# VectorE and ScalarE in program order, and the bf16 identity from GpSimd, in a windowed-attention and mixture-of-depths kernel

## The chip, the cores and the metric

The kernel runs on one core of a Trainium2 chip. The metric is the device time of one execution in microseconds. The five engines are named as the profile names them: PE (TensorE, with PEld for its weight loads), DVE (VectorE), ACT (ScalarE), POOL (GpSimd) and SP (SyncE, which here only issues transfers).

## What is computed

Sliding-window attention with sink tokens, followed by a small expert layer that only the best-scored rows of each batch go through. Batch 4, 8 heads, sequence 768, head size 64, 4 sink tokens, window 128, 128 rows chosen per batch.

```python
def _attn_ref(q, k, v, n_sink, window):
    scores = scale * np.matmul(q, k.transpose(0, 1, 3, 2))
    ...
    keep = is_sink | in_window
    scores = np.where(keep, scores, -1000000000.0)
    ...
    a = a / (np.sum(a, axis=-1, keepdims=True) + 1e-09)
    return np.matmul(a, v).astype(np.float32)

def _moe_ref(x, w_gate, w1, w2, capacity):
    scores = np.einsum('bsd,d->bs', x, w_gate)
    out = x.copy()
    for b in range(B):
        top_idx = np.argpartition(-scores[b], capacity)[:capacity]
        xe = x[b, top_idx]
        h = np.maximum(xe @ w1, 0.0)
        ye = h @ w2
        g = 1.0 / (1.0 + np.exp(-scores[b, top_idx]))
        out[b, top_idx] = x[b, top_idx] + g[:, None] * ye
    return out.astype(np.float32)
```

`x` is the attention output with the heads side by side, 512 wide.

## The kernel before

**Units.** The main loop runs over 24 units, one for each batch b and block j of 128 query rows (`units`, six per batch). A unit u does the following in program order. At j == 0 the loads of the next batch are issued (`load_qk`, `load_v`), and at u0 those of three of the four weight pieces (`load_w`; the fourth at u6). Then `scores` for the *next* unit: PE multiplies K and Q (L257), adds the mask by a product with the bf16 identity (L268), and ACT takes the exponentials into `pt` (L274, four per unit). Then `pv_sinks` and `pv` for this unit: PE sums the products with V in PSUM tiles `xg` (L291, L301), in two halves of four heads, and DVE normalises each half (L307 reciprocal of the row sum, L310 multiplication into `x`). At j == 0 `sink_scores` (L280, L282) follows. `transposes` turns one or two head pairs of the next batch (PE L227, DVE copies KT at L232 and two small pieces ksk at L236, ACT copies QT at L234). In batch 1 `cast_w` casts two weight pieces per unit on ACT (L212, L215), in the units j = 0 to 3. `compare` ranks the *previous* unit: PE transposes its column of gate scores (L324), ACT copies it (L325), DVE counts (L328). One step of the generator `moe_steps` of the previous batch follows. Last comes `finish_block`: the store of `x` (L315) and the gate score of each row as a dot product on DVE (L317).

**The expert steps.** `moe_steps` of batch b runs spread over the units of batch b+1, one step per unit from j == 1: the ranks (L340, L344, L345), the selection matrix E (L347) and the row numbers (L352, L353); the indices (L359, L362), the gate (L364 to L366) and the gather of the chosen rows by an indirect transfer (L369); their transposition (L375, L377); the first product (L385, L387); the second product (L391, L394) and the indirect transfer that adds to the output (L395). For the last batch all steps run at the end, one after the other.

**Loads.** All loads and the stores of `x` are issued by SP. `load_v` has a DVE instruction in its middle: after the second of six pieces of V it loads the sink rows (`vsr`, L126, two small transfers) and multiplies them by a selection pattern into `vsk` (L127). For batch 0 this stands ahead of the main loop; for batches 1 to 3 it stands at the head of unit u0, u6 and u12. The casts of q and k to bf16 are made by ACT and DVE in batch 0 (L107, L108) and by POOL afterwards (L111, an affine_select that changes no value).

**Buffers.** `xg` has three PSUM buffers, two used per unit; the other PSUM tiles share five. `x` has four buffers, each free when its store has landed. The f32 tiles of q and k have three buffers per kind, two used per batch; the bf16 ones three. V has one buffer for even and one for odd batches.

**What sets the order.** The framework places each instruction in its engine's stream when the program is built. For an engine that is named in `manual_schedule` the instructions within that block keep the order of the program. For the others a planner takes, by its own estimate of times, the first instruction of the program whose inputs are ready. Before the change only PE is named, so DVE, ACT, POOL and SP are ordered by the planner. What stands ahead of the block (constants, masks, the loads of batch 0) is ordered by the planner in any case. On the chip each stream is executed as it stands.

The identity matrix exists twice: `ident_f` in f32, for the transposes of the gate scores (L324), and `ident_b` in bf16, for the other transposes and the masks. `make_identity` is a POOL memset followed by a POOL affine_select.

Of the kernel before, what the change touches and what calls it, by code (L numbers as in the profile page):

```python
# [10 lines left out]
BF16 = mybir.dt.bfloat16  # L11
# [4 lines left out]
ENG = mybir.EngineType  # L16
# [15 lines left out]
def kernel(  # L32
# [13 lines left out]
    nc = tc.nc  # L46

    cp = ctx.enter_context(tc.tile_pool(name="cp", bufs=1))
# [24 lines left out]
    def keep_warm(n):  # L73
        w = ps.tile([128, 512], FP32, name="w", tag="ps")
        for _ in range(n):
            nc.tensor.matmul(out=w[:, :], lhsT=warm[:, 0:128], rhs=warm[:, :], start=True, stop=True)
# [21 lines left out]
    def casts(st, hp):  # L98
        kb = qbp.tile([128, 2, NB, D], BF16, name="kb", tag="kb")
        qb = qbp.tile([128, 2, NB, D], BF16, name="qb", tag="qb")  # L100
        h0 = 2 * (hp % 2)
        ks = st.kf[hp // 2][:, h0:h0 + 2, :, :].rearrange("p h c d -> p (h c d)")
        qs = st.qf[hp // 2][:, h0:h0 + 2, :, :].rearrange("p h c d -> p (h c d)")
        ko = kb[:, :, :, :].rearrange("p h c d -> p (h c d)")
        qo = qb[:, :, :, :].rearrange("p h c d -> p (h c d)")
        if st.b == 0:
            nc.scalar.copy(out=ko, in_=ks)  # L107
            nc.vector.tensor_copy(out=qo, in_=qs)  # L108
        else:
            for o, i in ((ko, ks), (qo, qs)):  # L110
                nc.gpsimd.affine_select(out=o, in_=i, compare_op=ALU.is_ge, fill=0.0, base=0,  # L111
                                        pattern=[[0, 2 * NB * D]], channel_multiplier=0)
        st.kq[hp] = (kb, qb)
# [17 lines left out]
    st0 = load_qk(0, 2)  # L131


    ident_f = cp.tile([128, 128], FP32, name="ident_f", tag="ident_f")
    make_identity(nc, ident_f)
    ident_b = cp.tile([128, 128], BF16, name="ident_b", tag="ident_b")
    nc.vector.tensor_copy(ident_b[:], ident_f[:])  # L137
    for i in range(2):
        nc.vector.memset(vsr[i][:, :], 0.0)
        nc.vector.memset(ksk[i][:, :, :], 0.0)  # L140
# [60 lines left out]
    def load_w(i):  # L201
        if i < 2:
            src = moe_w1[256 * i:256 * i + 256, :].rearrange("(dc p) f -> p dc f", p=128)
        else:
            src = moe_w2[512 * (i - 2):512 * (i - 2) + 512, :].rearrange("(fc p) d -> p fc d", p=128)
        wf[i] = ws.tile([128, 2048], FP32, name="wf", tag="wf")
        nc.sync.dma_start(out=wf[i][:, :].rearrange("p (a n) -> p a n", a=src.shape[1]), in_=src)  # L207
# [10 lines left out]
    def transposes(st, hp):  # L218
        if not hasattr(st, "QT"):
            st.QT = tp.tile([128, HP, S], BF16, name="QT", tag="QT")  # L220
            st.KT = tp.tile([128, HP, S], BF16, name="KT", tag="KT")
            st.ksk = ksk[st.b % 2]
        for t, (src, dst) in enumerate(((st.kq[hp][0], st.KT), (st.kq[hp][1], st.QT))):
            trp = ps.tile([128, 8, 128], BF16, name="trp", tag="ps")
            for c in range(NB):
                for e in range(2):
                    nc.tensor.transpose(out=trp[64 * e:64 * e + 64, c, :],  # L227
                                        in_=src[:, e, c, :], identity=ident_b[:])
            o = dst[:, hp, :].rearrange("d (p c) -> d p c", c=NB)
            i = trp[:, 0:NB, :].rearrange("d c p -> d p c")  # L230
            if t == 0:
                nc.vector.tensor_copy(out=o, in_=i)  # L232
            else:
                nc.scalar.copy(out=o, in_=i)  # L234
        for e in range(2):
            nc.vector.tensor_copy(  # L236
                out=st.ksk[64 * e:64 * e + 64, hp, 8 * (hp % 2) + 4 * e:8 * (hp % 2) + 4 * e + 4],
                in_=st.KT[64 * e:64 * e + 64, hp, 0:NSINK])
# [6 lines left out]
    def scores(st, kc, g):  # L245
        nq = 256 if kc + 1 < NB else 128
        if g == 0:
            st.pt[kc] = pp.tile([128, H, 256], FP32, name="pt", tag="pt")
        pt = st.pt[kc]
        sc = [ps.tile([128, 2, 256], FP32, name="sc", tag="ps") for _ in range(2)]  # L250
        for hh in range(2):
            hp = 2 * g + hh
            for kh in range(2):
                k0 = kc * 128 + 64 * kh
                q0, q1 = (64, nq) if kh else (0, nq if kc == 0 else min(nq, 192))
                for e in range(2):
                    nc.tensor.matmul(  # L257
                        out=sc[e][es[kh], hh, q0:q1], lhsT=st.KT[es[e], hp, k0:k0 + 64],
                        rhs=st.QT[es[e], hp, kc * 128 + q0:kc * 128 + q1],
                        start=(hh == 0), stop=False, skip_group_check=True)  # L260
        sq = [((2, 4), (0, 2)), ((0, 1), (3, 4))] if nq == 256 else [((0, 1), (0, 2))]
        for r, pair in enumerate(sq):
            for kh in range(2):
                s0, s1 = pair[kh]
                m0 = 2 if (s0, s1) == (0, 1) else 1 if s0 == 0 else 0
                m = msk0 if kc == 0 and kh == 0 else msk
                for e in range(2):
                    nc.tensor.matmul(  # L268
                        out=sc[e][es[kh], :, 64 * s0:64 * s1].rearrange("p h (s n) -> p h s n", n=64),
                        lhsT=ident_b[es[e], es[e]], rhs=m[es[e], :, m0:m0 + s1 - s0, :],  # L270
                        start=False, stop=(r == len(sq) - 1), skip_group_check=True)
        po = pt[:, 4 * g:4 * g + 4, :].rearrange("p (a e) n -> p e a n", e=2)
        for e in range(2):
            nc.scalar.activation(out=po[:, e, :, 0:nq], in_=sc[e][:, :, 0:nq], func=ACT.Exp, scale=0.125)  # L274
# [125 lines left out]
    def start_state(st):  # L400
        st.pt = {}
        st.cm = {}
        st.scol = sp.tile([128, NB], FP32, name="scol", tag="scol")
        st.row = sp.tile([128, NB], FP32, name="row", tag="row")
        st.sbc = sp.tile([128, S], FP32, name="sbc", tag="sbc")

    states = {0: st0}
    units = [(b, j) for b in range(B) for j in range(NB)]
    with tc.manual_schedule(engines={ENG.PE}):
        start_state(st0)  # L410
        keep_warm(14)
        for g in range(2):
            for hp in (2 * g, 2 * g + 1):
                casts(st0, hp)
                transposes(st0, hp)
                keep_warm(4)
            scores(st0, 0, g)
        gen = None
        prep = {True: {2: (0,), 3: (1, 2), 4: (3,)}, False: {1: (0,), 2: (1,), 3: (2,), 4: (3,)}}
        for u, (b, j) in enumerate(units):  # L420
            st = states[b]
            if j == 0 and b + 1 < B:
                states[b + 1] = load_qk(b + 1, 2 if b == 0 else 1)
                load_v(states[b + 1])
                if b == 0:
                    for i in range(3):
                        load_w(i)
            nxt = units[u + 1] if u + 1 < len(units) else None
            if nxt:
                if nxt[1] == 0:  # L430
                    start_state(states[nxt[0]])
                for g in range(2):
                    scores(states[nxt[0]], nxt[1], g)
            pv_sinks(st, j)
            hps = prep[b == 0].get(j, ()) if b + 1 < B else ()
            for hp in hps:
                casts(states[b + 1], hp)
            for g in range(2):
                pv(st, j, g)
            if j == 0:  # L440
                sink_scores(st)
            for hp in hps:
                transposes(states[b + 1], hp)
            if b == 1 and j < 4:
                cast_w(2 * j)
                cast_w(2 * j + 1)
                if j == 0:
                    load_w(3)
            if u:
                pb, pj = units[u - 1]  # L450
                compare(states[pb], pj)
            if gen is not None:
                if next(gen, "end") == "end":
                    gen = None
            finish_block(st, j)
            if j == 0 and b > 0:
                gen = moe_steps(states[b - 1])
        compare(states[B - 1], NB - 1)
        for _ in moe_steps(states[B - 1]):
            pass  # L460
# [35 lines left out]
```

The softmax here doesn't subtract the row's maximum and nothing guards it: scores larger than these inputs give would overflow.

## Time and profile before

The time is 171.62 us, the median of three runs (170.14 to 174.56). The profiled execution has a span of 173.3 us.

| engine | busy us | share of the span |
|---|---|---|
| PE (matmul) | 129.0 | 74% |
| DVE | 96.8 | 56% |
| ACT | 87.4 | 50% |
| POOL | 35.1 | 20% |

The DMA engines move 31.67 MB. No engine is busy for the whole span, so the shares do not name a bound: the table of windows, which gives busy time, granted PE clock and DMA share by stretch, and the chain of waits, which follows the last instruction back through what released it, are the views to read. Two groups matter for the change. ACT spends 46.8 us in 96 exponentials. DVE spends 20.3 us in the multiplications of L310, 17.4 in the dot products of L317, 17.9 in the counts of L328 and 15.1 in the copies of L232; the sink multiplication L127 runs four times at 0.42 us.

In the chain, 16% of the span is PE in L301; 24% is waiting for transfers.

### The profile page before, as it was taken

The numbers are of one execution on the slowest core, as the hardware profiler recorded it, in microseconds if no ns is written. First come the engines' busy times: TensorE is split into PE (matmuls) and PEld (weight loads), VectorE is DVE, ScalarE is ACT, GpSimd is POOL, SyncE is SP. The second block draws the span as 40 slices with busy tenths as digits, with TensorE's granted clock in tenths as the row PEclk, the third lists the DMA queues.
The fourth block names the chain that finished last, engine by engine and source line by source line (L and its number), as shares of the span: only waits on it lengthen the run. The fifth ranks groups of instructions, "written<-read, shape, count | busy, mean of one in ns | idle before, by whom it ended". The sixth has DMA issues, their size and how long they took to land.

```text
span 173.3 us, 6858 instructions
## 1 busy us (share of the span) xinstructions
PE 129.0 (74%) x3010; PEld 99.4 (57%) x3010; DVE 96.8 (56%) x303; ACT 87.4 (50%) x173; POOL 35.1 (20%) x51
## 2 busy tenths in 40 slices
PE   7379977589409979644999899999999699512930
PEld 2145666377207768532986678788678588201800
DVE  3188453977204999861277689775678735720000
ACT  3256873644593854646074855658585543101210
POOL 6000027600001616300541330200210200310030
PEclk9999999999755999996599999999999999955585
DMA  5999999899999799999869971311161411142004
GB/s 178 296 338 200 148 333 371 180 222 313 297 377 333 219 345 185 168 348 379 299 211 229 209 213 61 46 60 64 64 121 64 99 61 66 61 61 30 0 0 61
DMA packets 40078, 31.67 MB, mean 183 GB/s; under 512 B 26096, under 2 KB 34800, under 8 KB 40048
## 3 DMA queue, kind: packets, MB, share of 16 engines
q1 hardware_dynamic: 38896, 29.66, 59.3%
q0 software_dynamic: 1152, 1.57, 6.7%
q8 instruction: 23, 0.38, 0.9%
q14 instruction: 7, 0.06, 0.1%
HBM read 24.41 MB, written 7.34 MB: 183 GB/s over the span
## 4 chain that ended last, share of the span: by engine, by line
PE 35%; DMA 24%; DVE 13%; SPq 12%; issue 9%; ACT 2%; POOLq 1%
PE xg L301 16%; DMA xe<-out_dram,idx 9%; DMA qf<-in_q_dram 8%; DMA out_dram<-x 7%; SPq L120 6%; PE xg L291 3%; PE sc L257 3%; PE hps L385 3%; PE ye L391 3%; DVE x L310 3%; DVE KT L232 3%; SPq L126 2%; DVE cm L328 2%; SPq L207 2%; PE sc L268 2%
## 5 line engine op out<-in xcount | busy, mean ns | idle before, releaser
L274 ACT ACTIVATE pt<-sc 128x512 f32<-128x512 f32 (+1 forms) x96 | 46.8, 578 | 10.6 <-PE sc L268 10.5
L301 PEld LDWEIGHTS xg<-vbuf,pt 128*64 128x64 f32 x1408 | 46.1, 144 | 9.0 <-issue 7.0
L301 PE MATMUL xg<-vbuf,pt 128*64 128x65 f32 x1408 | 49.7, 231 | 0.6 <-PE xg L301 0.6
L307 DVE RECIPROCAL rz<-xg 128x4 f32<-128x4 f32 x48 | 8.7, 181 | 32.6 <-PE xg L301 32.5
L310 DVE TENSOR_TENSOR x<-xg,rz 128x256 f32<-128x256 f32 x48 | 20.3, 424 | 9.0 <-DMA out_dram<-x 7.4
L257 PE MATMUL sc<-QT,KT 64*64 64x192 bf16 (+3 forms) x384 | 19.3, 250 | 6.6 <-DVE KT L232 3.4
L234 ACT COPY QT<-trp 128x768 bf16<-128x768 bf16 x16 | 12.7, 799 | 22.1 <-PE trp L227 22.1
L111 POOL TENSOR_SCALAR_AFFINE_SELECT kb<-kf 128x768 bf16<-128x768 f32 x12 | 10.2, 865 | 63.6 <-DMA kf<-in_k_dram 37.9
L268 PE MATMUL sc<-msk,ident_b 64*64 64x256 bf16 (+1 forms) x352 | 17.3, 248 | 3.2 <-issue 3.2
L328 DVE SCALAR_TENSOR_TENSOR cm<-sbc,scol,tie 128x128 bf16<-128x128 f32 (+5 forms) x24 | 17.9, 747 | 2.9 <-ACT sbc L325 2.7
L317 DVE CUSTOM_DVE_ANT_0 junk<-x,wgb 128x512 f32<-128x512 f32 x24 | 17.4, 726 | 2.3 <-DMA wgb<-in_moe_w_gate_dram 2.2
L257 PEld LDWEIGHTS <-KT 64*64 64x64 bf16 x384 | 9.5, 107 | 12.6 <-issue 10.0
L291 PE MATMUL xg<-vsk,psk 64*64 64x260 f32 x128 | 12.6, 416 | 5.2 <-DVE x L310 5.2
L232 DVE COPY KT<-trp 128x768 bf16<-128x768 bf16 x16 | 15.1, 950 | 1.0 <-PE trp L227 0.9
L395 POOL DMA_INDIRECT out_dram<-gye,idx x4 | 6.4, 1589 | 42.3 <-DMA out_dram<-x 15.4
L268 PEld LDWEIGHTS <-ident_b 64*64 64x64 bf16 x352 | 10.8, 109 | 3.7 <-issue 3.7
L325 ACT COPY sbc<-bc 128x128 f32<-128x128 f32 x24 | 6.5, 271 | 12.5 <-PE bc L324 12.5
L111 POOL TENSOR_SCALAR_AFFINE_SELECT qb<-qf 128x768 bf16<-128x768 f32 x12 | 10.8, 915 | 6.1 <-PE xg L301 3.3
L227 PE MATMUL trp<-ident_b,kb 128*64 128x128 bf16 x192 | 8.7, 223 | 4.1 <-DVE ident_b L137 3.8
L375 PE MATMUL xeT<-ident_b,xe 128*128 128x128 bf16 x16 | 2.0, 264 | 11.9 <-DMA xe<-out_dram,idx 11.9
L227 PEld LDWEIGHTS <-kb 128*64 128x64 bf16 x192 | 6.8, 113 | 5.6 <-issue 5.0
L385 PE MATMUL hps<-xeT_sb,w_sb 128*128 128x128 bf16 x128 | 9.4, 242 | 0.7 <-ACT xeT_sb L377 0.7
(72 smaller groups left out, 138.9 us busy)
## 6 DMA issues: line engine op xcount, KB each, us to landing
vbuf<-in_v_dram SPq DMA_DIRECT2D x24, 256.0 KB, 5.6
out_dram<-x SPq DMA_DIRECT2D x24, 256.0 KB, 5.3
wf<-in_moe_w_dram SPq DMA_DIRECT2D x4, 1024.0 KB, 7.8
kf<-in_k_dram SPq DMA_DIRECT2D x8, 384.0 KB, 8.8
qf<-in_q_dram SPq DMA_DIRECT2D x8, 384.0 KB, 8.4
kf<-in_k_dram SPq DMA_DIRECT2D x4, 768.0 KB
qf<-in_q_dram SPq DMA_DIRECT2D x4, 768.0 KB, 4.8
wgb<-in_moe_w_gate_dram SPq DMA_DIRECT2D x1, 256.0 KB
```

Source lines behind the costliest of these rows:

```text
L111: nc.gpsimd.affine_select(out=o, in_=i, compare_op=ALU.is_ge, fill=0.0, base=0, pattern=[[0, 2 * NB * D]], channel_multiplier=0)
L227: nc.tensor.transpose(out=trp[64 * e:64 * e + 64, c, :], in_=src[:, e, c, :], identity=ident_b[:])
L232: nc.vector.tensor_copy(out=o, in_=i)
L257: nc.tensor.matmul(out=sc[e][es[kh], hh, q0:q1], lhsT=st.KT[es[e], hp, k0:k0 + 64], rhs=st.QT[es[e], hp, kc * 128 + q0:kc * 128 + q1], sta ...
L268: nc.tensor.matmul(out=sc[e][es[kh], :, 64 * s0:64 * s1].rearrange("p h (s n) -> p h s n", n=64), lhsT=ident_b[es[e], es[e]], rhs=m[es[e], ...
L274: nc.scalar.activation(out=po[:, e, :, 0:nq], in_=sc[e][:, :, 0:nq], func=ACT.Exp, scale=0.125)
L291: nc.tensor.matmul(out=st.xg[g][es[m], :, :], lhsT=st.psk[es[g], q0:q0 + 64], rhs=st.vsk[es[g], :, :], start=True, stop=False, skip_group_ ...
L301: nc.tensor.matmul(out=xg[es[m], hh, :], lhsT=st.pt[kc][:, h, off + 64 * m:off + 64 * m + 64], rhs=st.v[:, kc, h, :], start=(j < 2 and hh ...
L310: nc.vector.tensor_tensor(out=st.x[:, 256 * g:256 * g + 256].rearrange("p (h d) -> p h d", h=4), in0=xg[:, :, 0:D], in1=rz[:, :, :].to_bro ...
L317: nc.vector.tensor_tensor_reduce(out=junk[:, :], in0=st.x[:, :], in1=wgb[:, :], scale=1.0, scalar=0.0, op0=ALU.mult, op1=ALU.add, accum_ou ...
L328: nc.vector.scalar_tensor_tensor(out=cm[:, :], in0=st.sbc[:, 0:n], scalar=st.scol[:, j:j + 1], in1=tie[:, S - n:S], op0=ALU.subtract, op1= ...
L385: nc.tensor.matmul(out=hps[:, f4, :], lhsT=w1_sb[:, dc, f0:f0 + 128], rhs=xeT_sb[:, dc, :], start=(dc == 0), stop=(dc == 3))
```

## The change

Two edits. The bf16 identity is now built by POOL itself, ahead of the f32 one, and the DVE cast that made it is gone. And DVE and ACT join PE in `manual_schedule`: within the prologue of batch 0 and the main loop they execute their instructions in the order in which the program has them. The aim is that the author, and not the planner's estimate, says which copy, count or exponential goes first; the identity is built elsewhere so that the first transposes don't depend on where a DVE cast is placed. No arithmetic changes.

```diff
@@ -131,10 +131,10 @@
     st0 = load_qk(0, 2)
 
 
+    ident_b = cp.tile([128, 128], BF16, name="ident_b", tag="ident_b")
+    make_identity(nc, ident_b)
     ident_f = cp.tile([128, 128], FP32, name="ident_f", tag="ident_f")
     make_identity(nc, ident_f)
-    ident_b = cp.tile([128, 128], BF16, name="ident_b", tag="ident_b")
-    nc.vector.tensor_copy(ident_b[:], ident_f[:])
     for i in range(2):
         nc.vector.memset(vsr[i][:, :], 0.0)
         nc.vector.memset(ksk[i][:, :, :], 0.0)
@@ -406,7 +406,7 @@
 
     states = {0: st0}
     units = [(b, j) for b in range(B) for j in range(NB)]
-    with tc.manual_schedule(engines={ENG.PE}):
+    with tc.manual_schedule(engines={ENG.PE, ENG.DVE, ENG.Activation}):
         start_state(st0)
         keep_warm(14)
         for g in range(2):
```

## The prediction

> **What bounds the kernel now.** I call the 24 blocks of work units u0 to u23 (u0 to u5 are batch 0, u6 to u11 batch 1, and so on) and hp0 to hp3 the head pairs. I read the table of windows first, because the shares of the page mix three stages.
>
> ```profile
> 20.00:24.00 4.00, 4.00 (x126) 3.32 (x120) 1.45 (x5) 3.96 (x9) 0.00 (x0) 1.00 0.91 215
> 45.50:52.30 6.80, 1.56 (x24) 0.72 (x14) 0.51 (x2) 6.66 (x10) 0.00 (x0) 0.50 1.00 329
> 75.50:80.30 4.80, 0.05 (x2) 0.02 (x2) 2.14 (x7) 2.78 (x4) 0.00 (x0) 0.93 1.06 339
> 80.30:86.40 6.10, 6.10 (x108) 5.13 (x110) 0.75 (x3) 1.74 (x5) 2.17 (x3) 0.50 0.95 344
> 98.00:126.00 28.00, 27.22 (x741) 22.46 (x729) 21.09 (x68) 17.92 (x40) 4.15 (x4) 1.00 0.34 90
> 155.00:173.30 18.30, 6.67 (x44) 4.70 (x44) 0.00 (x0) 2.47 (x4) 2.57 (x2) 0.59 0.17 21
> ```
>
> The columns are stretch, length, busy time of PE, PEld, DVE, ACT and POOL, granted clock, DMA share, GB/s. Up to about 86 us the DMA engines are full (shares near 1) and PE twice stands still (45.5 to 52.3 and 75.5 to 80.3). From 98 to 126 PE is busy for 27.2 of 28 us: there PE is the bound, in program order already. The last 18 us are a serial tail. The chain of waits names the two halts:
>
> ```profile
> 39.33 12.44 DMA out_dram<-x
> 51.79 0.44 DVE x L310
> ...
> 71.61 8.63 DMA xe<-out_dram,idx
> 80.29 0.61 PE xeT L375 x4
> ```
>
> The normalisation of u4 (L310) waits for a buffer of x until the store of u0 has landed, behind 3 MB of weights; and PE waits for the gathered rows of batch 0 until 80.29. Then I read VectorE's timeline for the one instruction that stands in another place in the program than in this trace, the sink-value multiplication L127:
>
> ```profile
> 20.30 0.18 DVE L307 RECIPROCAL rz<-xg 128x4 f32<-128x4 f32 x1 [1.98 <-PE xg L301]
> ...
> 36.55 0.41 DVE L127 TENSOR_TENSOR vsk<-vsr,sel 128x256 f32<-128x256 f32 x1
> ...
> 60.12 0.17 DVE L307 RECIPROCAL rz<-xg 128x4 f32<-128x4 f32 x1
> ...
> 68.88 0.41 DVE L127 TENSOR_TENSOR vsk<-vsr,sel 128x256 f32<-128x256 f32 x1
> ```
>
> In the program, L127 of batch b+1 comes at the head of the first unit of batch b, ahead of that unit's L307. Here it runs 16 us after u0's L307 (batch 1) and 9 us after u6's (batch 2). SyncE's timeline says why:
>
> ```profile
> 28.83 3.37 SPq L126 DMA_DIRECT2D vsr<-in_v_dram  x2
> 62.75 2.21 SPq L126 DMA_DIRECT2D vsr<-in_v_dram  x2
> ```
>
> Its input is issued at 28.8 and 62.8; the completion events of the trace stand at 33.9 and 67.2.
>
> **What the Trainium skill says.** "Perfetto Trace Analysis", Tensor Engine Instruction: "ACT/DVE/GPSIMD are strict FIFO". The trace agrees: the cast L137, whose input was ready at 1.5 us, ran at 9.57 behind a cast that waited for q, and PE's transposes waited 3.8 us for it. "TensorE: Matmul & The Clock Gate", Part 1: an idle window of about 3.4 us halves PE's clock, and about 3.4 us of work restores it. Here 4.8 us of idleness is followed by a clock of 0.50 for 6.1 us. "DMA: Bandwidth & Descriptors", Queues, rings and completion order: an engine takes the descriptors of a ring in order. Here a 256 KB store took 12.44 us behind the weights and 2.0 us at the least.
>
> **The change, part by part.**
>
> Identity. One VectorE cast of 0.22 us (L137) goes; a POOL memset (0.20 us) and affine_select come (0.28 us for f32, 0.295 us for bf16 of this size in L179). POOL idles from 4.2 to 24.9 us, so they cost nothing. PE's wait of 3.8 us for L137 goes: the transposes of hp0 start near 6.5 instead of 9.84. But ScalarE's program order gives it back: the k cast of hp2 ran at 9.95, and now stands behind the exponentials of hp0 and hp1. Step by step: q cast of hp1 ends 9.5; transposes and QT copy (0.80) to 11.0; scores and two exponentials (1.09) to 12.7; k cast (0.83) 13.5; transposes 14.3; QT 15.1; the same for hp3, 17.5. The last scores of u0 start at 17.84 now. Saved: 0.3 us.
>
> L127 of batch 1. VectorE stops at about 18 and goes on at 34.0. Behind it are u0's two reciprocals and multiplications, so x of u0's first half comes at 34.0 + 0.42 + 0.18 + 0.42 = 35.05 instead of 20.9. PE has three xg buffers: it does half of u1 and stops at about 23.5, so it restarts at half clock. From there, with the unit lengths of the trace (5 to 6 us in this stage, the first one slow): second halves of u1 36.7, u2 41.8, u3 47.8, u4 53.3, u5 58. Before they were 24.8, 29.9, 36.5, 41.9, 56.6. So a stop of 14 us arrives as about 1.5 us, because u4 had to wait until 51.79 for the store of u0, which still lands then (issued 39.3, x of u0 is ready).
>
> L127 of batch 2. u6 could be normalised from about 61; VectorE is held until vsr has landed. If SyncE's order stays, the loads stand behind the store of u5, 1.5 us later, and land at 68.6. But stores of u3 to u5 become ready later than the loads of batch 2, whose buffers are free early, and the planner that orders SyncE takes what is ready: then vsr lands one unit earlier, about 64.5. I take 64.5; 68.6 is the other end. With 64.5 the first x of u6 comes at 65.1 instead of 60.75, and PE, ready for it at 63.5, idles 1.6 us: too short for the clock.
>
> Weight casts. The eight ScalarE casts (1.06 us each) ran at 46.6 to 53.4 and 77.2 to 79.2, in idle time. In program order two stand in each of u6 to u9 behind the QT copy and ahead of the copy sbc (L325). So cm, and the dot product (L317) after it, come 2.1 us later, and the next unit's PE transpose of the scores waits for L317: 0 to 2 us in each of u7 and u8, once they run at PE's pace. I take 2 us in all.
>
> Gather of batch 0. u7 ends at 66.2, u8 at 71.2, u9 at 77.3; idx is ready at 77 instead of 71.3. The gather then needs 3.3 us (the least seen) to 8.6 us; the weights that held it (landed 77.1) are through, but loads of batch 3 can be ahead. I take 5: xeT at 82, against 80.29. PE idles under 3.4 us before it, so it is not slowed; from xeT to the end of u10 the slow clock took 5.97 us, the same stage of batch 2 3.88 (111.79 to 115.67). That is 2.1 us back.
>
> Rest. Units from u10 on stand in nearly the same order on both engines. E comes ahead of the two small rid operations and L317 after E: about 0.4 us in u14, and 0.4 in the tail, where the two rid operations (0.18 and 0.17 plus gaps) leave idle time and join the path.
>
> Sum: +1.7 at xeT, -2.1 for the clock, +0.4 +0.4 = +0.4 us. 171.6 + 0.4 = 172.0.
>
> **The rivals.** (1) SyncE's order stays and the second stop is paid in full: vsr at 68.6, first x of u6 at 69.7, PE idle for 6 us and then at half clock; u7 71.3, u8 77.7, u9 82.7, gather issued at 82.4, xeT at 86.4: +6.1 - 2.1 + 0.8 = +4.8, so 176.4. For it: the stores are queued in order and VectorE is late; against it: batch 2's buffers are free early. (2) Faster: the loads of batch 2 come early enough that L127 of batch 2 hardly holds, PE keeps its own pace and the gather finds empty queues: xeT at 79.0, weight casts hidden: -1.3 - 2.1 + 0.4 = -3.0, 168.6. For it: DMA is full from 2 to 86 us whatever VectorE does; against it: the idx chain starts late. Much more isn't to be had, since xeT to end is PE and tail in both.
>
> **How the numbers follow.** Forecast 0.5, slower rival 0.37, faster rival 0.13. The range takes in both rivals: down to 168.5, just under the faster sum, and up to 177.5, a gather of 1 us more in the first rival. Over 2% faster means under 168.2, a little beyond the second rival: 0.1. Over 2% slower means above 175.05, the first rival nearly whole: 0.35. The rest is 0.55.
>
> **What would show it.** In the new timeline: the transposes of hp0 at 6.5; VectorE idle from 18 to 34 with L127 at its end, released by the vsr load; PE idle from 23.5 to 35; u5's second half at 58; a second halt before L127 of batch 2, between 61 and 64 to 69; weight casts in pairs between 60 and 85; the wait for xe shorter than 3.4 us and the clock 1.0 after it. The forecast is wrong if L127 does not hold VectorE, if SyncE's order puts stores of batch 0 ahead of the loads of batch 2, or if units after u10 become longer.

## The result and the profile after

The changed kernel takes 185.02 us (median, 183.46 to 186.77). The kernel before took 172.19 us on the same chip, so the ratio is 1.077 with a 95% interval of 1.059 to 1.095. It is slower, and the forecast of 172.0 (168.5 to 177.5) is wrong. Executions of one kernel fall into a fast and a slow group, and the ratios here and below compare fast ones alone, so they differ a little from the quotient of the medians.

The profiled execution of the changed kernel took 186.8 us, at the upper end of its times. A second profiled execution of the same kernel took 181.0. Where the two differ I give both, so that nothing rests on the one alone. The profiled execution of the kernel before took 175.05 us, the upper end of its own times, so moments in the traces lie less far apart than the medians, above all for the second execution.

I read the table of windows first again. The columns are stretch, length, busy time of PE, PEld, DVE, ACT and POOL (with the number of instructions), granted clock, DMA share and GB/s. Before:

```profile
18.00:34.00 16.00, 11.86 (x348) 9.40 (x342) 8.88 (x27) 9.92 (x21) 7.04 (x8) 1.00 0.95 262
34.00:64.00 30.00, 21.90 (x553) 17.21 (x546) 17.09 (x52) 18.42 (x34) 3.53 (x5) 0.83 0.97 299
64.00:80.00 16.00, 9.18 (x269) 7.71 (x268) 12.35 (x36) 8.35 (x16) 4.94 (x5) 0.99 1.03 251
```

After:

```profile
18.00:34.00 16.00, 7.80 (x164) 5.39 (x164) 1.36 (x4) 6.29 (x12) 4.96 (x6) 0.74 0.99 277
34.00:64.00 30.00, 23.41 (x541) 19.60 (x541) 17.61 (x54) 11.29 (x24) 5.65 (x7) 0.80 0.96 301
64.00:80.00 16.00, 12.67 (x353) 10.26 (x357) 11.94 (x37) 12.88 (x23) 2.70 (x3) 1.00 0.91 239
```

From 18 to 34 VectorE executes 4 instructions instead of 27 (7 in the second execution), and PE 164 matmuls instead of 348 (164 there too). From 34 to 64 PE makes up nothing here: 541 against 553. It no longer halts for the store of u0, but it has other waits, and the clock is no better (0.80 against 0.83). In the second execution it makes up a little, with 609 at a clock of 0.89. By 64 us, 705 and 773 matmuls stand against 901. From 64 to 80 it regains some of it. Then it stands still for the gathered rows, for 8.6 us in the first execution and 4.0 in the second, against 4.75 before. From the transposes of the gathered rows (L375) to the end, the old trace has 93.0 us and the new ones 90.8 and 91.6. So the whole loss lies ahead of L375, in the first half of the kernel: L375 starts at 94.35 (87.74 in the second execution) instead of 80.29.

VectorE's waits name the first cause (columns: who waits for whom, us in total, times, longest):

```profile
DVE vsk L127 <- DMA vsr<-in_v_dram: 22.4, 3, 15.1
DVE cm L328 <- ACT sbc L325: 5.9, 6, 1.7
```

The second execution has three such waits as well, 20.4 us in all. The chain of waits of the first, with start and length of each piece (SPq is SyncE at work on an issue, a DMA piece the time until a transfer has landed), goes through that wait twice, and then through the gather:

```profile
29.86 1.69 SPq L126
31.60 2.79 DMA vsr<-in_v_dram
...
34.48 0.43 DVE vsk L127
...
64.21 0.44 DVE x L310
64.66 0.36 SPq L315
...
66.26 3.15 DMA vsr<-in_v_dram
...
69.50 0.09 DVE vsk L127
...
82.21 5.68 issue
...
88.11 6.20 DMA xe<-out_dram,idx
```

In the second execution the chain goes through the wait for batch 1 too; in the place of the one for batch 2 it has weight casts, which are shown further down. The middle part is a loop between two in-order streams. VectorE waits in L127 for vsr; vsr stands in SyncE's stream behind the store of u5 (L315); that store waits for x of u5 (L310), which VectorE made late because of the first stop. SyncE's timeline shows the same thing one store earlier. Before:

```profile
39.33 2.30 SPq L315 DMA_DIRECT2D out_dram<-x  x4
41.72 0.96 SPq L93 DMA_DIRECT2D kf<-in_k_dram  x1
```

In the changed kernel:

```profile
39.87 10.98 SPq L315 DMA_DIRECT2D out_dram<-x  x3
50.94 0.39 SPq L93 DMA_DIRECT2D kf<-in_k_dram  x1
65.54 1.35 SPq L126 DMA_DIRECT2D vsr<-in_v_dram  x2
```

In both kernels the first load of batch 2 stands behind the stores of u0 to u3. Before, their x was ready when SyncE came to them, and the load left at 41.72. Now the stores have to wait for their x, and it leaves at 50.94 (46.92 in the second execution).

### The profile page after: what moved, and what is told of

It reads as the page before. It is cut to its first block, busy times and chain, and to the rows that moved or that the text cites. A ratio compares the mean times of both kernels' runs of the same rounds, so it can differ in the third digit from the quotient of the medians.

```text
span 185.1 us, 6868 instructions
## 1 busy us (share of the span) xinstructions
PE 130.8 (71%) x3010; PEld 101.0 (55%) x3010; DVE 94.8 (51%) x302; ACT 87.1 (47%) x173; POOL 34.3 (19%) x53
## 4 chain that ended last, share of the span: by engine, by line
PE 35%; DMA 25%; issue 12%; DVE 11%; SPq 9%; ACT 4%; POOLq 1%; POOL 0%; DVEq 0%
PE xg L301 17%; DMA xe<-out_dram,idx 9%; DMA qf<-in_q_dram 8%; SPq L120 4%; DMA kf<-in_k_dram 4%; PE xg L291 3%; DMA vsr<-in_v_dram 3%; PE sc L257 3%; PE hps L385 3%; PE ye L391 3%; DVE x L310 3%; DVE KT L232 2%; ACT pt L274 2%; SPq L126 2%; PE sc L268 2%
## 5 line engine op out<-in xcount | busy, mean ns | idle before, releaser
L301 PE MATMUL xg<-vbuf,pt 128*64 128x65 f32 x1408 | 50.8, 234 | 10.2 <-DVE rz L307 9.6
L301 PEld LDWEIGHTS xg<-vbuf,pt 128*64 128x64 f32 x1408 | 47.1, 148 | 18.6 <-issue 16.7
L274 ACT ACTIVATE pt<-sc 128x512 f32<-128x512 f32 (+1 forms) x96 | 46.6, 578 | 8.7 <-PE sc L268 8.7
L257 PE MATMUL sc<-QT,KT 64*64 64x192 bf16 (+3 forms) x384 | 20.0, 261 | 7.5 <-issue 2.3
L310 DVE TENSOR_TENSOR x<-xg,rz 128x256 f32<-128x256 f32 x48 | 20.4, 424 | 1.7
L268 PE MATMUL sc<-msk,ident_b 64*64 64x256 bf16 (+1 forms) x352 | 18.1, 257 | 2.3 <-issue 2.3
L325 ACT COPY sbc<-bc 128x128 f32<-128x128 f32 x24 | 6.5, 272 | 21.8 <-PE bc L324 21.8
L375 PE MATMUL xeT<-ident_b,xe 128*128 128x128 bf16 x16 | 2.0, 265 | 16.4 <-DMA xe<-out_dram,idx 16.4
L127 DVE TENSOR_TENSOR vsk<-vsr,sel 128x256 f32<-128x256 f32 x4 | 1.7, 424 | 22.4 <-DMA vsr<-in_v_dram 22.4
L268 PEld LDWEIGHTS <-ident_b 64*64 64x64 bf16 x352 | 11.4, 115 | 2.7 <-issue 2.7
L291 PE MATMUL xg<-vsk,psk 64*64 64x260 f32 x128 | 11.4, 413 | 0.0
L111 POOL TENSOR_SCALAR_AFFINE_SELECT qb<-qf 128x768 bf16<-128x768 f32 x12 | 10.1, 850 | 4.3 <-DMA qf<-in_q_dram 4.2
L76 PE MATMUL w<-warm 128*128 128x512 bf16 x30 | 10.0, 485 | 1.3 <-DVE warm L71 1.3
L227 PE MATMUL trp<-ident_b,kb 128*64 128x128 bf16 x192 | 8.2, 220 | 3.3 <-ACT kb L107 3.3
```

Of the source, the lines that this page charges most:

```text
L257: nc.tensor.matmul(out=sc[e][es[kh], hh, q0:q1], lhsT=st.KT[es[e], hp, k0:k0 + 64], rhs=st.QT[es[e], hp, kc * 128 + q0:kc * 128 + q1], sta ...
L268: nc.tensor.matmul(out=sc[e][es[kh], :, 64 * s0:64 * s1].rearrange("p h (s n) -> p h s n", n=64), lhsT=ident_b[es[e], es[e]], rhs=m[es[e], ...
L291: nc.tensor.matmul(out=st.xg[g][es[m], :, :], lhsT=st.psk[es[g], q0:q0 + 64], rhs=st.vsk[es[g], :, :], start=True, stop=False, skip_group_ ...
L301: nc.tensor.matmul(out=xg[es[m], hh, :], lhsT=st.pt[kc][:, h, off + 64 * m:off + 64 * m + 64], rhs=st.v[:, kc, h, :], start=(j < 2 and hh ...
L310: nc.vector.tensor_tensor(out=st.x[:, 256 * g:256 * g + 256].rearrange("p (h d) -> p h d", h=4), in0=xg[:, :, 0:D], in1=rz[:, :, :].to_bro ...
```

## The experiments

**The theories.** Theory 1: VectorE in program order stops at L127 until vsr has landed; all behind it, the normalisation of the batch's first unit above all, stops too, and SyncE's stores then hold back the next batch's loads. Theory 2: part of the loss is the late gather, because the planner, with other streams to fit, chose another order for GpSimd. Theory 3: ScalarE's program order puts the pairs of weight casts (L212, L215) ahead of the copies of the comparison (L325) and the next exponentials (L274). Theory 4: the identity edit itself delays something. Every ratio below is to the kernel before on the same chip, with its 95% interval.

**The change taken apart.** Three kernels: the identity edit alone, then with VectorE by hand, then with ScalarE by hand instead.

```diff
 e1:    with tc.manual_schedule(engines={ENG.PE}):
 e2:    with tc.manual_schedule(engines={ENG.PE, ENG.DVE}):
 e3:    with tc.manual_schedule(engines={ENG.PE, ENG.Activation}):
```

Identity alone:

> Only the identity edit, TensorE alone in order by hand as before. Theory 1 (the in-place order of VectorE makes L127 stop everything queued behind it until the slow loads of its batch land, and SyncE's stores then hold up the next batch's loads) expects 171 to 173 us, as before. Theory 4 (the identity built by GpSimd delays the start or GpSimd's casts) expects 175 us or more.

VectorE's order:

> Identity edit, TensorE and VectorE by hand, ScalarE left to the planner. Theory 1 expects nearly the whole loss: 182 to 186 us, with waits of L127 for vsr of about 4, 15 and 3 us. Theory 3 (ScalarE's order, with the weight casts ahead of the casts of the comparison, makes the loss) expects 172 to 176 us. Theory 2 (the late gather on GpSimd, a side effect of the planner's new order there) expects about 180 us if the gather is issued at once after its indices.

ScalarE's order:

> Identity edit, TensorE and ScalarE by hand, VectorE left to the planner. Theory 1 expects 171 to 174 us. Theory 3 expects 176 us or more, with waits of L328 for the casts of L325 of about 6 us in all.

Measured: identity alone 0.995 (0.989 to 1.001), VectorE's order 1.030 (1.017 to 1.042), ScalarE's order 0.980 (0.967 to 0.992). Theory 4 falls. VectorE's order alone costs, with the waits of the changed kernel in its trace, though the wait for batch 0 is missing:

```profile
DVE vsk L127 <- DMA vsr<-in_v_dram: 16.0, 2, 14.5
```

But it costs 3.0% and not the 7.7% of the whole, so theory 1 as I had put it ("nearly the whole loss") explains less than half of it by itself. ScalarE's order alone costs nothing and may gain a little. The two together cost 4.6% more than VectorE's alone: an interaction, which none of my theories had foreseen.

**L127 called later.** Its loads and its arithmetic stay; only its place in VectorE's stream moves behind the unit whose x it used to hold up.

```diff
-                nc.vector.tensor_tensor(
-                    out=st.vsk[:, :, 0:D], in0=raw[:, :].unsqueeze(1)...
+    def sink_values(st):
+        nc.vector.tensor_tensor(
+            out=st.vsk[:, :, 0:D], in0=vsr[st.b % 2][:, :].unsqueeze(1)...
...
             finish_block(st, j)
+            if u == 0:
+                sink_values(st)
+            if j == NB - 1 and b + 1 < B:
+                sink_values(states[b + 1])
```

> All of the change, but the multiply of L127 is called later: at the end of the first unit for batch 0, and at the end of a batch's last unit for the next batch. Theory 1 expects 170 to 174 us: the VectorE waits for vsr fall to under 2 us in all, second half of unit 5 done near 56 to 58 as before. Theory 2 expects 176 to 179 us (the 5 us gap ahead of the gather stays), theory 3 the same 176 to 179 us with L328 still waiting for L325.

Measured: 1.017 (1.004 to 1.029), 177.2 us. The waits for vsr are gone, and 6 of the 7.7% with them, but not all. VectorE's timeline of this kernel (start, length, line, operation; in brackets the idle time before it and what ended it) shows what took their place; line numbers here are 2 higher, so L312 is the multiplication into x:

```profile
44.21 0.18 DVE L309 RECIPROCAL rz<-xg 128x4 f32<-128x4 f32 x1 [0.36 <-PE xg L303]
53.09 0.42 DVE L312 TENSOR_TENSOR x<-xg,rz 128x256 f32<-128x256 f32 x1 [8.70 <-DMA out_dram<-x]
...
53.98 0.95 DVE L234 COPY KT<-trp 128x768 bf16<-128x768 bf16 x1
```

It is x of u4 waiting for the store of u0, the very wait that bound the kernel before. There the planner had let the copies of KT and a comparison run ahead of the waiting multiplication:

```profile
41.94 0.18 DVE L307 RECIPROCAL rz<-xg 128x4 f32<-128x4 f32 x1 [0.75 <-PE xg L301]
42.26 0.96 DVE L232 COPY KT<-trp 128x768 bf16<-128x768 bf16 x1
43.26 0.34 DVE L236 COPY ksk<-KT 64x4 bf16<-64x4 bf16 x2
43.63 0.75 DVE L328 SCALAR_TENSOR_TENSOR cm<-sbc,scol,tie 128x512 bf16<-128x512 f32 x1
...
51.79 0.76 DVE L310 TENSOR_TENSOR x<-xg,rz 128x256 f32<-128x256 f32 x2 [7.40 <-DMA out_dram<-x]
```

In program order KT stands behind it, and PE's scores wait 7.5 us for KT. Theory 1 has to be widened: not L127, but whatever VectorE instruction comes to a transfer first.

**Is it the wait or the place?** L127 stays where it is and reads a tile of zeros that is ready from the start; the sinks' values are left out of the output.

```diff
+    still = vp.tile([128, D], FP32, name="still", tag="still")
+    nc.vector.memset(still[:, :], 0.0)
-                    out=st.vsk[:, :, 0:D], in0=raw[:, :].unsqueeze(1)...
+                    out=st.vsk[:, :, 0:D], in0=still[:, :].unsqueeze(1)...
```

> All of the change, L127 left where it stands in VectorE's order, but it multiplies a tile of zeros that is there from the start instead of vsr (the sinks' part of the values is left out of the output; the loads of vsr stay). Theory 1 (what stands behind L127 is held by the wait and not by the place) expects 176 to 178 us, as with the late multiply, with no VectorE wait for vsr, and the wait of x of unit 4 for the store of unit 0 in its place. If the place or the altered order of SyncE is the cause, 182 to 185 us.

Measured: 1.023 (1.014 to 1.032), 176.5 us, the same as with the late call, and x of u4 again waits 8.4 us for the store. So what costs is the wait, not the place. The planner did give SyncE a slightly other order here (fewer loads of batch 2 ahead of the store of u4), but vsr of batch 2 stands behind the store of u5 in this kernel as in the changed one.

**L127 late for batch 1 only.** As the late call, but only for batch 1, whose stop is the longest (15.1 us).

```diff
+                if b != 1:
+                    sink_values(st)
...
+            if j == NB - 1 and b == 0:
+                sink_values(states[b + 1])
```

> All of the change, with L127 called late for batch 1 only. Theory 1 with the stop of batch 1 (15 us of wait) as the main one expects unit 5 done near 60 instead of 64 and 178 to 181 us; the stops of batch 0 (4.1 us) and batch 2 (3.2 us) stay. If the late gather and the order of ScalarE make most of the loss, 183 to 185 us.

Measured: 1.060 (1.050 to 1.069), 182.2 us. Taking away the longest stop alone was worth 1.7%, and the intervals overlap. u5 is done at 56.7, as in the kernel before and 7.5 us sooner than in the changed one (3.6 sooner than in its second execution); but the vsr of batch 2 lands at 65.4 all the same, L127 of batch 2 now holds VectorE for 4.83 us (here it stands at L116), and u6 is normalised at 66.6. A stop ahead of a transfer that is late anyway is only moved.

**GpSimd by hand too.**

```diff
-    with tc.manual_schedule(engines={ENG.PE, ENG.DVE, ENG.Activation}):
+    with tc.manual_schedule(engines={ENG.PE, ENG.DVE, ENG.Activation, ENG.Pool}):
```

> All of the change, with GpSimd in order by hand too, so the first gather stands ahead of the casts for batch 3. Theory 2 (5 us of the loss are the late gather, which comes from the order that the planner chose for GpSimd) expects the gather within 0.5 us of its indices, the first transposes of the gathered rows near 89 instead of 94.4, and 179 to 181 us. If the gather is late for another reason, 184 to 186 us.

Measured: 1.071 (1.064 to 1.078), 184.0 us, though the gather is issued 0.3 us after its indices. The changed kernel once more, for a second trace:

> The changed kernel once more, unaltered, for a second trace. If the late first gather is a property of the kernel, 5 us again lie between the indices of L362 and the gather of L369; if it came from the moment at which that one execution stood, 0.3 us as in every other run. The time is 182 to 187 us in either case.

Measured: 181.0 us for the profiled execution, 183.6 as the median of two. GpSimd's timeline of the first trace has the gather like this,

```profile
88.11 1.12 POOL L369 DMA_INDIRECT xe<-out_dram,idx  x1 [5.57 <-DMA qf<-in_q_dram]
```

and that of the second like this:

```profile
81.30 1.23 POOL L369 DMA_INDIRECT xe<-out_dram,idx  x1 [3.18 <-DVE gt L366]
```

The indices were written at 82.89 and 80.35. The gap of 5.2 us belongs to one execution; in the other it is 0.95. The order of GpSimd is not a cause of the loss, and theory 2 falls. Why that one gather stood for 5.2 us with its inputs written is open: the program waits there for nothing that had not arrived (the load of q in the bracket is what the cast next in the stream waits for). One thing in the two traces would fit. In both, GpSimd's stream goes on (at 87.89 and 81.30) 1.6 us after a transfer of 8 KB of the kind "instruction" has ended, at 86.27 in the first and at 79.69 in the second. No run tested whether it waits for that transfer.

**The weight casts out of the way.** In the changed kernel, six of the eight casts move to units 3 to 5, where ScalarE has room. L127 stays in place.

```diff
-            if b == 1 and j < 4:
-                cast_w(2 * j)
-                cast_w(2 * j + 1)
-                if j == 0:
-                    load_w(3)
+            if b == 1 and j == 0:
+                load_w(3)
+            if b == 1 and j == 3:
+                cast_w(6)
+                cast_w(7)
...
             finish_block(st, j)
+            if b == 0 and j > 2:
+                cast_w(2 * j - 6)
+                cast_w(2 * j - 5)
```

> All of the change, with six of the eight weight casts called in units 3 to 5 of batch 0, where ScalarE has room, and only the last two in unit 9. Theory 3 (of the 5.6 us that the two orders together cost beyond VectorE's alone, most is the pairs of 2.0 us casts that stand ahead of the exponentials in units 6 to 9) expects 179 to 182 us. If that share comes from elsewhere, 184 to 186 us.

Measured: 1.031 (1.021 to 1.042), 179.1 us: 4.6% less, and within 0.2% of what VectorE's order costs alone (1.030). So the interaction is the weight casts, and theory 3 holds for that share. ScalarE's timeline of the changed kernel shows the mechanism,

```profile
67.64 0.60 ACT L282 ACTIVATE psk<-sk 128x512 f32<-128x512 f32 x1 [0.43 <-PE sk L280]
68.13 1.98 ACT L212 CAST w_sb<-wf 128x1024 bf16<-128x1024 f32 x2
70.01 0.27 ACT L325 COPY sbc<-bc 128x128 f32<-128x128 f32 x1
70.17 2.08 ACT L274 ACTIVATE pt<-sc 128x512 f32<-128x512 f32 x4
72.39 0.80 ACT L234 COPY QT<-trp 128x768 bf16<-128x768 bf16 x1
73.09 1.99 ACT L212 CAST w_sb<-wf 128x1024 bf16<-128x1024 f32 x2
```

and the chain of its second execution has the casts on the path three times before the gather:

```profile
65.80 1.05 ACT w_sb L212
66.84 0.17 ACT sbc L325
67.01 1.96 ACT pt L274 x4
...
70.45 1.10 ACT w_sb L212
...
77.69 1.89 ACT w_sb L215 x2
79.58 0.18 ACT sbc L325
79.78 0.49 DVE cm L328 x2
80.28 0.08 DVE idx L362
```

**Both causes taken away.** L127 late and the casts early.

> All of the change, with the late multiply of L127 (alone 7.8 us less) and with six weight casts in units 3 to 5 (alone 5.9 us less). If these two are the whole loss and add up, 170 to 173 us. If they overlap (both act through the same transfers of the first 80 us), 173 to 177 us. Above 177 us the casts cost only where L127 stops VectorE.

Measured: 1.0095 (1.001 to 1.018), 174.8 us. Of the 7.7%, 6.8 are gone. Alone the two edits took 6.0 and 4.6, so they overlap. With L127 in place the casts are worth 4.6%, with L127 late only 0.7% (1.017 to 1.0095, with overlapping intervals). My reading, argued and not shown for itself: once L127 has pushed the units of batch 1 back, PE finds its data landed there and everything ScalarE adds counts; without the stop the same units still wait for transfers, and the casts lie beside that.

**The wait for the store.** What is left is x of u4 behind the store of u0, and that store is behind 3 MB of weights. First the weights are issued in unit 3 instead of unit 0, on top of the late L127:

```diff
-                if b == 0:
-                    for i in range(3):
-                        load_w(i)
+            if b == 0 and j == 3:
+                for i in range(3):
+                    load_w(i)
```

> The late multiply, and the first three weight loads issued in unit 3 instead of unit 0, so the stores of units 0 to 2 go ahead of them. Theory 1, widened (any VectorE instruction in order by hand that waits for a DMA stops all behind it; without L127 it is x of unit 4, which waits 8.7 us for the store of unit 0 behind 3 MB of weights), expects that wait under 2 us, unit 4 done near 45 instead of 53.6, and 168 to 173 us. If the loads of batch 2 bound the first batches in any case, 175 to 178 us.

Measured: 172.5 us (median, but spread from 166.7 to 176.5, so no interval and no verdict) beside 171.6 of the kernel before. In the trace, of an execution of 174.4 us, VectorE's wait for the store is gone, u4 is done at 44.1 and u5 at 48.8, 8 us ahead of the kernel before; yet u8 is done at 69.6 and there at 69.9. The weights now stand ahead of the loads of batch 2, the first of which leaves at 49.68. The lead is lost again: both readings of the expectation had a part.

So the weights have to go behind the loads of batch 2. In three kernels (the one before, the one with ScalarE by hand, and the one with L127 late) they are loaded from unit 6 on and cast in units 8 to 11:

```diff
-                if b == 0:
-                    for i in range(3):
-                        load_w(i)
...
-            if b == 1 and j < 4:
-                cast_w(2 * j)
-                cast_w(2 * j + 1)
-                if j == 0:
-                    load_w(3)
+            if b == 1 and j == 0:
+                for i in range(3):
+                    load_w(i)
+            if b == 1 and j > 1:
+                cast_w(2 * j - 4)
+                cast_w(2 * j - 3)
+                if j == 2:
+                    load_w(3)
```

The kernel before with late weights:

> The kernel before, with the first three weight loads called in unit 6 instead of unit 0, the fourth in unit 8, and their casts in units 8 to 11 instead of 6 to 9. If the store of unit 0 behind 3 MB of weights (12.4 us on the chain of before) costs the kernel before time of its own, unit 5 is done near 47 instead of 56.7 and the time is 164 to 169 us. If the loads of the first two batches bound it as a whole, 170 to 173 us.

ScalarE by hand with late weights:

> Identity edit, TensorE and ScalarE by hand (169.6 us), with the weights late as in the run of before with late weights. If the wait for the store of unit 0 costs time of its own, 161 to 167 us. If the loads bound the first batches as a whole, 168 to 171 us.

All of the change, L127 late, with late weights:

> All of the change with the late multiply of L127 (177.2 us), and the weights late as well. Theory 1, widened, expects that nothing is left of the loss once no VectorE instruction waits long for a DMA: the same as the run with ScalarE by hand and late weights, within 2 us. If the in-order VectorE costs something of its own, it stays 4 us or more above that run.

Measured: 0.956 (0.947 to 0.965), 167.4 us; 0.963 (0.954 to 0.973), 166.9 us; 0.977 (0.969 to 0.985), 169.7 us. The place of the weights, which is that of their loads and, two units later than before, of their casts, is worth 4.4% to the kernel before; no run moved the loads without the casts. In the windows of the kernel before with late weights,

```profile
18.00:34.00 16.00, 12.40 (x345) 9.56 (x348) 9.47 (x29) 10.59 (x21) 6.77 (x8) 1.00 0.96 276
34.00:64.00 30.00, 26.69 (x733) 22.39 (x730) 25.04 (x70) 16.01 (x35) 6.80 (x9) 0.94 0.94 261
```

PE executes 733 matmuls from 34 to 64 instead of 553, at a DMA share of 0.94 instead of 0.97. The transfers were not the bound as a sum; their order was. And once no VectorE instruction waits long for a transfer, the change with all its in-order streams is faster than the kernel before as it was. It is not faster than the kernel before with late weights, its fair partner: there it is 2.3 us behind, and the intervals lie apart. It stays 2.8 us behind the kernel with ScalarE alone by hand, which is neither the 2 us that theory 1 allowed nor the 4 us of its rival. So a smaller cost of the program order seems to remain, though against the kernel with ScalarE by hand the intervals just overlap. Its cause stays open. The chain of this kernel goes through a load of weights of 6.43 us that ends at a weight cast, but ScalarE waited for it only 0.17 us (line numbers are 2 higher):

```profile
63.63 1.99 ACT L214 CAST w_sb<-wf 128x1024 bf16<-128x1024 f32 x2 [0.17 <-DMA wf<-in_moe_w_dram]
```

The best of all are the kernel before and the one with ScalarE by hand, each with late weights; their intervals overlap.

## Why the prediction was wrong

**Identity: right.** PE's first transposes start at 6.34 and 7.0 in the two executions (forecast 6.5), and the edit alone is 0.995 with 1 inside the interval, as the -0.3 us of the working had it.

**"L127 of batch 1": mechanism right, its size off.** VectorE executes L127 at 34.48 after 15.07 us of idleness (forecast: from 18 to 34.0) and x of u0 starts at 35.03 (forecast 35.05). PE stops at 26.0 (forecast 23.5) and resumes at 35.60. The second halves of u1 and u2 are done at 37.8 and 42.2, within 1.1 us of the forecast. Then the step fails: the unit lengths of the old trace, "5 to 6 us in this stage", held for neither execution. u3, u4 and u5 ended at 50.0, 55.8 and 64.2 in one and at 46.0, 55.0 and 60.3 in the other, against 47.8, 53.3 and 58. In each execution one or two of these units take about 8 to 9 us: a wait of 1.5 to 2.9 us that ends in what the profile calls "issue", then L301 at half clock (3.2 to 3.6 instead of 2.0 us for 64 matmuls). The chain of the first execution, at u3:

```profile
43.96 1.45 issue
...
46.21 3.61 PE xg L301 x64
```

and that of the second, at u4:

```profile
48.71 1.54 issue
...
51.31 3.50 PE xg L301 x64
```

The "issue" waits are not new: the kernel before has three of them from 25 to 46 us (1.49, 1.72 and 1.99 us), so its unit lengths already hold them. New is the clock of 0.50 in these units: after the first two waits of the kernel before L301 took 2.09 us, at a clock of 1.00, and only after the third, at 45.5, did the clock fall. The working counted an idleness of 1.6 us, and at the gather anything under 3.4, as too short for the clock; here waits of 1.45 and 2.31 us in one execution and 2.88 in the other were followed by 3.4 us at 0.50. Why the clock falls after some of these waits and not after others is open. The term put at +1.5 us measured +3.6 and +7.5 at u5.

What the "issue" waits are, the traces hint at. In the 16 traces of this case, every such wait of PE above 0.7 us, 40 in all, ends 1.1 to 1.8 us after a transfer of 16 KB of the kind "instruction" (queue q8) has ended; the one above ends at 45.41, its transfer at 43.97. That points to PE waiting for its own instructions. No run varied it.

**L127 of batch 0: missed.** I looked for the stops at units u0, u6 and u12. The prologue's L127 is called ahead of the ordered block, so the planner still chooses its place, and in the changed kernel it put it ahead of the KT copies of the last head pairs. There it held VectorE for 4.1 us (3.6 in the second execution), and the last scores of u0 start at 20.31 and 19.34 instead of 17.84. No run took this stop away alone, but little of it can have come through: PE then stood until L127 of batch 1 in any case, and in the kernel with L127 late for batch 1 only, where a stop of 2.9 us for batch 0 remains, u5 is done at 56.7 as before.

**"L127 of batch 2": the step on SyncE was wrong.** I let the planner move loads of batch 2 ahead of stores of batch 0 so far that vsr lands one unit earlier, and took 64.5 with 68.6 as the other end. The planner did move four of them forward, two ahead of the store of u4 and two ahead of that of u5, but not vsr, which stands behind the store of u5 as before. And the first load of batch 2 stands behind the store of u3 as before, where the late x now held it: it left 9.2 us later, 5.2 in the second execution. L127 ran at 69.50 in one execution and 65.61 in the other, so the truth reached past my other end once. Stores of batch 0 ahead of the loads of batch 2 were what I had named as making the forecast wrong, and the unchanged place of vsr was the rival at 0.37.

**"Weight casts": 2 us, measured 7.9.** The order and the path were as described, but the casts delay the four exponentials of the next unit too, not only the copy L325 and the dot product behind it, and they lie on the chain of the second execution in three units, not two. 4.6% of 172 us is 7.9 us with L127 in place; with L127 late it is 0.7%, 1.3 us. A price that depends so much on another edit's effect can't be added as a constant.

**"Gather of batch 0".** idx was ready at 82.9 and 80.4 instead of 77, late with the units ahead of it. The gather took 6.2 and 6.4 us to land, not 5, and in one execution stood 5.2 us before that. PE waited 8.6 and 4.0 us, both above the 3.4 us that the forecast stayed under, so the clock was slow after it, and of the 2.1 us that I gave back only 1.3 and 1.0 came (4.7 and 4.9 us from L375 to the end of u10, instead of 5.97).

**"Rest": right as a sum, by luck.** From L375 to the end 90.8 and 91.6 us; the forecast's terms give 93.0 - 2.1 + 0.8 = 91.7. But only 1.3 and 1.0 of the 2.1 came, and from the end of u10 on the changed kernel was 1.0 and 0.4 us shorter, not 0.8 longer. The two errors cancel.

So the forecast put L375 at 82 and it came at 87.74 and 94.35. Two terms failed in size: the stop of L127 of batch 1, which was to arrive as 1.5 us, and the weight casts at 2 us, worth 7.9 us where L127 stops VectorE. With both taken away 6.8 of the 7.7% are gone. The first rival had the right story for batch 2 and nearly the right moment, L375 at 86.4 against 87.74 in the second execution; it fell short in the same two terms. My working hid the first stop behind u4's wait for a store that "still lands then". The runs say that this wait and L127 are stops in the same in-order stream: with L127 out of the way it is u4's wait that stops VectorE, for 8.7 us. As I read them, the slack of one stage, once used for the first stop, was no longer there for the casts and for the loads; no run shows that for itself.

## What to carry to other kernels

When an engine is taken from a planner and put into program order, list every instruction in its stream that reads what a transfer brings or writes a buffer that a store must free; each is a place where the whole engine stops, and taking the first away uncovers the next. Either move these instructions behind the work that feeds others, or order the transfers so that they have landed by then. A transfer queue that mixes stores with loads closes the loop: the late engine delays its stores, and these delay the loads that it will wait for.

## What I had not expected

ScalarE in program order costs nothing alone (0.980) and 4.6% beside VectorE's (1.030 to 1.077). The weights' place, a matter of which transfer is called first and not of how many bytes, is worth 4.4% of the kernel before, although its DMA engines show a share of 0.97 in the stretch. And two executions of one kernel can differ by 5 us in a single issue (the gather, 5.2 and 0.95 us after its indices), so a gap in one trace needs a second trace before it is called a cause. And a wait of PE of 1.45 us was followed by 3.4 us at half clock.
